# Block-sparse attention with an MLP behind it: the first batch's attention on float32 operands, and a planner with new numbers

## The chip, the core and the metric

The kernel runs on one core of a Trainium2 chip. The metric is device microseconds of one execution. The engines are TensorE (PE in the profile, with its weight loads as PEld), VectorE (DVE), ScalarE (ACT), GpSimd (POOL) and SyncE (SP), whose queue issues nearly all transfers.

## The reference

```python
scores = scale * np.matmul(q, k.transpose(0, 1, 3, 2))          # 4 batches, 8 heads, 768 positions, 64 wide
mask = |block_i - block_j| <= 1, first and last block row and column, 3 sampled blocks per block row
attn = softmax(np.where(mask, scores, -1e9))
attn_out = np.matmul(attn, v)
x = attn_out.transpose(0, 2, 1, 3).reshape(3072, 512)
h = x @ w_in                                                    # 512 x 2048
g = h * np.tanh(softplus(h))
return (g @ w_out).astype(np.float32)                           # 2048 x 512
```

A block has 32 positions, so a batch has 24 block rows. q, k and v are float32; the two weights arrive as 8-byte floats.

## The kernel before, in words

**Products in parts.** Every float32 operand of a large product is split into two float16 parts, a high one and a low one of what the high one leaves, after scaling by a power of two. A product is then three float16 products: high by high, low by high, high by low. The scale comes from a sum of squares: for the first batch from matmuls of a tile with itself (`gram`, L318) whose diagonal DVE picks (L333), for later batches from ACT squares (L309); a float32 matmul with a matrix of ones (`root_pe`, L344) sums over partitions, and DVE makes the scale (`root`, L349 and L352). `parts` writes the high part on ACT (L441) and the low part on DVE (L445).

**Attention.** A batch is 13 jobs: 11 of two sparse block rows each, and two dense ones (first and last block row). Per job: scores into PSUM (`scores`, L564; weights are 64x32 pieces of q, so eight such pieces lie side by side in the array), row maxima on DVE (L602 to L607), exponentials on ACT (L630), transposes on PE (L650), the transposed weights as high part on ACT (`ph`, L653) and low part on DVE (`pl`, L657), the product with v (`o_fn`, L679; 128x32 weights), then division (L698 to L701), a transpose (L708), and the parts of x (`xh` L726, `xl` L729). A sparse block row needs its keys gathered on POOL (`gather_k`, L504) and its values gathered by transfers (`gather_v`, L520 to L527) from `vd`, a copy of v in parts in device memory that `store_v` writes (L461). There are two value buffers (`vg`), so SP issues a gather when the block row two before it is done.

**Weights.** `w_in` comes in 8 transfers (`wr`), `w_out` in 16 (`wor`), all issued by SP (L745). DVE turns the 8-byte words into float32 with three integer operations per piece (L753, L756, L759). All of `w_out` has to be there before its one scale can be made (`scale_o`: `gram_wo`, `tp_wo`, `iv_o`); only then are its parts made (`parts_o`: `wt` L851 on DVE or L849 on ACT, high part L854 on ACT, low part L856 on POOL).

**MLP.** For 256 tokens `moe_h` (L895) makes h in groups of 12 matmuls and `moe_y` (L954) makes y in groups of 6. Between them lie `hs`, `us` and `g` (L904 to L939). The MLP has 192 groups of each; they are spread between the jobs. The first y group needs parts of `w_out`.

**What sets the order.** Every step is a `Task` with a planned duration, a priority `key` (smaller goes first) and a planned transfer time. `Plan.emit` (L85) plays the plan forward when the program is built and writes each engine's instructions in the order that it found; on the chip each engine then runs its list in that order. `pace` (L1099) holds a job's scores back: the first ones to the times in `START`, later ones so that the MLP keeps pace, with `RES` of it left for the end.

## Time and profile before

| | |
|---|---|
| three runs | 800.21, 801.33, 801.36 us |
| median | 801.33 us |
| profiled execution, span | 802.7 us (the page gives no time for it beside the span) |
| PE busy | 730.1 us, 91% of the span |
| DVE, ACT, POOL busy | 520.2, 536.2, 335.2 us |
| mean granted PE clock | 0.953 |
| moved | 94.22 MB |

Busy time is the time in which at least one instruction of a group is running, so groups that overlap in time add up to more than their engine's busy time. The mean of one matmul includes the time in which it overlaps its neighbours. "wr" and "wor" are raw pieces of the two weights, "raw_k" and so on raw tiles of the inputs.

### The profile page before, as it was taken

To read this page: it belongs to the slowest core of one execution; us is meant where nothing else is said; L and a number is where in the kernel's file an instruction comes from. 1 tells how busy PE (TensorE), PEld (TensorE's weight loads), DVE (VectorE), ACT (ScalarE), POOL (GpSimd) and SP (SyncE) were. 2 spreads that over 40 slices of the span, in tenths; PEclk is the share of its full clock that TensorE was granted. 3 is DMA by queue.
4 is the path that set the end of the run, shared out by engine and by line. 5 is a ranking of instruction groups with operands and counts; after the bars stand their busy time and mean duration, and the time that the engine had idled before them with its cause. 6 is when DMAs were issued, how large, how long until landed. Compare 5 with 4: busy or idle time off the path is not lost.

```text
span 802.7 us, 30250 instructions
## 1 busy us (share of the span) xinstructions
PE 730.1 (91%) x12626; PEld 515.6 (64%) x12626; DVE 520.2 (65%) x910; ACT 536.2 (67%) x836; POOL 335.2 (42%) x403
## 2 busy tenths in 40 slices
PE   4666678975999999999999999999999999999997
PEld 3544566763566757777677767677677767666653
DVE  6996777989786766767665666686767654323220
ACT  2556545777886748887777786886878766465650
POOL 2467540558674532434332543453545431302031
PEclk9956669997999999999999999999999999999999
DMA  8849557531304345526414264255243243100000
GB/s 286 311 136 242 148 151 228 185 108 41 120 36 148 87 112 156 144 88 188 135 57 121 79 173 138 69 148 151 61 128 93 80 136 89 39 14 14 15 14 26
DMA packets 56972, 94.22 MB, mean 117 GB/s; under 512 B 8067, under 2 KB 20356, under 8 KB 56836
## 3 DMA queue, kind: packets, MB, share of 16 engines
q1 hardware_dynamic: 56640, 92.03, 37.9%
q8 instruction: 99, 1.62, 0.9%
q14 instruction: 37, 0.30, 0.1%
q10 hardware_dynamic: 196, 0.27, 0.1%
HBM read 79.32 MB, written 12.95 MB: 115 GB/s over the span
## 4 chain that ended last, share of the span: by engine, by line
PE 72%; DVE 12%; DMA 7%; SPq 3%; issue 3%; ACT 2%; POOLq 0%; POOL 0%; DVEq 0%; ACTq 0%
PE y L954 28%; PE h L895 26%; PE t L650 6%; PE o L679 5%; PE s L564 5%; DMA wor<-in_moe_w_out_dram 2%; DMA wr<-in_moe_w_in_dram 1%; DVE wt L851 1%; SPq L527 1%; DMA vg<-vd 1%; PE tx L708 1%; DVE mx L607 1%; DVE wo L756 1%; DVE wi L756 1%; DMA vt<-vd 1%
## 5 line engine op out<-in xcount | busy, mean ns | idle before, releaser
L895 PE MATMUL h<-xh,wi 128*128 128x256 f16 x1536 | 286.6, 276 | 7.9 <-ACT hs L904 7.9
L954 PE MATMUL y<-wo,g 128*128 128x512 f16 x1152 | 278.4, 381 | 1.5 <-POOL g L939 0.9
L895 PEld LDWEIGHTS <-wi 128*128 128x128 f16 x2304 | 224.6, 99 | 61.2 <-issue 12.2
L895 PE MATMUL h<-xl,wi 128*128 128x256 f16 x768 | 211.5, 275 | 1.4 <-issue 1.4
L939 POOL TENSOR_TENSOR g<-hs,g 128x1024 f16<-128x1024 f32 x48 | 107.6, 2242 | 233.7 <-DVE g L936 146.0
L954 PEld LDWEIGHTS <-g 128*128 128x128 f16 x1152 | 110.3, 98 | 105.0 <-issue 5.1
L504 POOL COPY kg<-kt 128x256 f16 x264 | 121.5, 496 | 121.1 <-PE s L564 110.3
L904 ACT ACTIVATE hs<-h,gsc 128x512 f32<-128x512 f32 x96 | 65.6, 684 | 84.5 <-PE h L895 78.1
L630 ACT ACTIVATE pt<-s,nb,ns 128x256 f32<-128x256 f32 (+1 forms) x208 | 106.1, 579 | 8.0 <-PE t L650 4.0
L653 ACT ACTIVATE ph<-t 128x512 f16<-128x512 f32 x112 | 65.5, 593 | 62.9 <-PE t L650 50.3
L657 DVE SCALAR_TENSOR_TENSOR pl<-t,ph 128x512 f16<-128x512 f32 x112 | 76.0, 685 | 44.5 <-ACT ph L653 44.1
L928 DVE SCALAR_TENSOR_TENSOR hs<-us,hs 128x1024 f32<-128x1024 f32 x48 | 63.6, 1324 | 44.0 <-ACT us L927 42.2
L650 PE MATMUL t<-ident,pt 128*128 128x128 f32 x448 | 76.9, 299 | 12.9 <-ACT pt L630 5.8
L650 PEld LDWEIGHTS t<-ident,pt 128*128 128x128 f32 x448 | 56.1, 152 | 23.4 <-issue 4.8
L924 POOL TENSOR_TENSOR us<-us 128x1024 f32<-128x1024 f32 x23 | 46.9, 2041 | 54.7 <-DVE us L922 50.1
L679 PEld LDWEIGHTS <-ph 128*32 128x32 f16 x3584 | 50.7, 97 | 25.2 <-issue 19.9
L607 DVE TENSOR_REDUCE mx<-s 128x4 f32<-128x1024 f32 x44 | 53.4, 1213 | 7.4 <-PE s L564 7.3
L922 DVE TENSOR_SCALAR us<-us 128x1024 f32<-128x1024 f32 x48 | 38.8, 809 | 28.7 <-ACT us L918 28.6
L918 ACT ACTIVATE us<-hs,hsc 128x1024 f32<-128x1024 f32 x48 | 55.2, 1149 | 1.0
L926 ACT ACTIVATE us<-us 128x1024 f32<-128x1024 f32 x48 | 50.6, 1055 | 4.5 <-POOL us L924 3.8
L564 PEld LDWEIGHTS <-q 64*32 64x32 f16 x2976 | 35.6, 99 | 27.4 <-issue 22.3
L679 PE MATMUL o<-vg,ph 128*32 128x65 f16 (+1 forms) x3072 | 51.2, 201 | 2.1 <-DMA vg<-vd 2.0
(179 smaller groups left out, 895.3 us busy)
## 6 DMA issues: line engine op xcount, KB each, us to landing
...
wor<-in_moe_w_out_dram SPq DMA_DIRECT2D x16, 512.0 KB, 4.1
...
raw_k<-in_k_dram SPq DMA_DIRECT2D x12, 512.0 KB, 5.6
raw_q<-in_q_dram SPq DMA_DIRECT2D x12, 512.0 KB, 3.9
raw_v<-in_v_dram SPq DMA_DIRECT2D x12, 512.0 KB, 4.9
```

The lines of the kernel that those rows point to most:

```text
L504: nc.gpsimd.tensor_copy(out=kgs[n][:, :, c0:c0 + BS], in_=tl["kt", b][:, :, ds(j, BS)])
L564: nc.tensor.matmul(s[g][i * BS:(i + 1) * BS, c0 + cs.start:c0 + cs.stop], q[gs, c * NPR + i, qs], src[gs, a * NPR + i, ks], start=first an ...
L630: ex = lambda o, x, g, w: nc.scalar.activation(out=o, in_=x, func=AF.Exp, bias=nb[:, g, w:w + 1], scale=tl["ns", b, sus[w]["qb"] // TB][:, ...
L650: nc.tensor.transpose(t[:, k, g], src, ident)
L653: nc.scalar.activation(out=new(sb, "ph", ("ph", i, j), [P, 2, 2, P], F16), in_=tl["t", i, j], func=AF.Copy, scale=PSC)
L657: nc.vector.scalar_tensor_tensor(out=new(sb, "pl", ("pl", i, j), [P, 2, 2, P], F16), in0=tl["t", i, j], scalar=PSC, in1=tl["ph", i, j], op ...
L679: nc.tensor.matmul(o[cs, w, g, 0:v1 - v0], p[:, k, g, cs], vt[:, k, 2 * c + g, v0:v1], start=j == 0 and g == 0 and k == 0 and n == 0, stop ...
L895: nc.tensor.matmul(h[:, f2].rearrange("p (s q) -> p s q", q=BS), wi[:, fp, w, cc, fs], x[:, :, cc], start=f2 == 0 and k == 0, stop=f2 == 1 ...
L904: nc.scalar.activation(out=tl[kq][:, 2 * (fp % 2):2 * (fp % 2) + 2], in_=tl[kh], func=AF.Copy, scale=gsc[:, fp:fp + 1])
L928: add("DVE", 1.32, lambda: nc.vector.scalar_tensor_tensor(out=hs(), in0=us(), scalar=-0.5, in1=hs(), op0=ALU.add, op1=ALU.mult), r=[ku], w ...
L939: add("POOL", 2.3, lambda: nc.gpsimd.tensor_tensor(out=g()[:, 1], in0=hs(), in1=g()[:, 0], op=ALU.subtract), r=[kq, ("gh", b, t, k)], w=[kg])
L954: nc.tensor.matmul(tl[ky], tl["g", b, t, k][:, g, f, q], wo[:, fc, w], start=fc == 0 and n == 0, stop=fc == NFC - 1 and n == 2)
```

## The change

For batch 0 alone (`exact`), K and Q go straight into the tiles that the scores read, as float32 (`load32`); nothing is summed, scaled or split for them, and a constant stands in for their scale (`ns0`). The scores of a job are then 32 float32 matmuls for a sparse job, where 96 float16 ones were. V is copied as float32 beside a column of ones (`copy_v`) and stored as float32; a block row of v has the same bytes as before. The transposed weights are copied once as float32 (`pp`, on ACT or DVE) instead of `ph` and `pl`, and o is 16 float32 matmuls for 48. The scale of V is still needed for the MLP; its sum of squares is on ACT now. Batches 1 to 3 compute as before. The planned transfer times are lower (1.5 for 2.2 us, 3.0 for 4.4 us, 0.65 for 0.9 us), nearly every `key` has another number, `RES` exceeds the planned duration of the whole MLP, so `pace` holds back only the 18 jobs in `START`.

```diff
-RINGS = dict(s=1, t=2, o=1, h=2, y=1, raw=6, wr=3, pt=2, ph=4, pl=4, xh=3, xl=3, mx=3, nb=3, r=2,
+RINGS = dict(s=1, t=2, o=1, h=2, y=1, raw=6, wr=3, pt=2, pp=4, xh=3, xl=3, mx=3, nb=3, r=2,
...
-    vd = [dram.tile([S + BS, H, VW], F16, name=f"vd{b}") for b in range(B)]
+    exact = lambda b: b == 0
+    vd = [dram.tile([S + BS, H, D + 1 if exact(b) else VW], F32 if exact(b) else F16, name=f"vd{b}") for b in range(B)]
...
+    def load32(what, j):
...
+        def fn():
+            if what == "q" or j == 0:
+                t = new(sb, "kt" if what == "k" else "q", key, [P, NPR * (S if what == "k" else TT)])
+                tl[("x32", *key)] = full(t, k=S if what == "k" else TT)
+            dst = tl[("x32", *key)]
+            dst = dst[:, :, js] if what == "k" else dst
+            nc.sync.dma_start(out=dst, in_=(kT if what == "k" else qT)[b, :, :, js].rearrange("r d s -> d r s"))
+        first = what == "q" or j == 0
+        add("SP", 0.5, fn, w=[(what, b, j)], new=[("kt" if what == "k" else "q", key)] if first else (),
+            use=[key] if key not in ((what, b, j),) else (), key=-35, lat=2.0, kind=("dma", 1.5))
...
-            kind=("dma", 2.2 * n))
+            kind=("dma", 1.5 * n))
...
         first = what == "q" or j == 0
-        if b == 0:
-            if what == "q" or j == NTT - 1:
-                js = [j] if what == "q" else T3
-                add_gram((what, b, j), [lambda j=j: tl["flat", what, b, j] for j in js], [("raw", what, b, j) for j in js],
-                         "h", lambda: new(sb, f"ss{what}", key, [P, NTT])[:, 0:1], [key], [(f"ss{what}", key)], cls)
-            return
...
+    def copy_v(j):
+
+        key, kr = ("v", 0, j), ("raw", "v", 0, j)
...
+        def fn(eng):
+            dst, src = tl[key][:, :, :, 0:D], tl[kr].rearrange("p c (h d) -> p c h d", d=D)
+            if eng == "ACT":
+                nc.scalar.activation(out=dst, in_=src, func=AF.Copy)
+            else:
+                (nc.vector if eng == "DVE" else nc.gpsimd).tensor_copy(out=dst, in_=src)
+        add("POOL", 0.3, ends, w=[("ends",) + key], new=[("raw", key)], use=[key], key=-9)
+        add("DVE", 0.8, lambda: fn("DVE"), r=[kr, ("ends",) + key], w=[key], use=[key], key=ATV + 10,
+            also=[("ACT", 1.16, lambda: fn("ACT")), ("POOL", 2.0, lambda: fn("POOL"))])
...
-            r=[("v", b, j)], w=[("vd", b, j)], key=-4, lat=2.5, kind=("dma", 2.4))
+            r=[("v", b, j)], w=[("vd", b, j)], key=-6, lat=2.5, kind=("dma", 1.7))
...
+                kt, kg = (tl["x32", "kt", b], kg32) if exact(b) else (tl["kt", b], kgs)
+                nc.gpsimd.tensor_copy(out=kg[n][:, :, c0:c0 + BS], in_=kt[:, :, ds(j, BS)])
+        add("POOL", 0.53 * NR, fn, r=KT3(b) + ["off"], w=[("kg", n)], use=[("kt", b)], key=8)
...
-        add("SP", 2.9, fn, r=VD3(b) + ["off", "z"], w=[("vg", n)], key=-3, lat=2.4, kind=("dma", 0.9))
+        add("SP", 2.9, fn, r=VD3(b) + ["off", "z"], w=[("vg", n)], key=-2, lat=2.4, kind=("dma", 0.65))
...
-    WHOLE = 12
+    WHOLE = 13
...
+        if exact(b):
+            q = tl["x32", "q", b, qb // TB]
+            for m, (cs, src, ks) in enumerate(pieces):
+                for i in range(NPR):
+                    for g in range(2):
+                        gs = slice(g * D, (g + 1) * D)
+                        nc.tensor.matmul(
+                            s[g][i * BS:(i + 1) * BS, c0 + cs.start:c0 + cs.stop], q[gs, i, qs], src[gs, i, ks],
+                            start=first and m == 0, stop=last and m == len(pieces) - 1)
+            return
...
+        def pp_fn(j, eng):
+            pp_new(j)
+            if eng == "ACT":
+                nc.scalar.activation(out=tl["p32", i, j], in_=tl["t", i, j], func=AF.Copy)
+            else:
+                nc.vector.tensor_copy(out=tl["p32", i, j], in_=tl["t", i, j])
...
-            add("ACT", 0.62, lambda j=j: ph_fn(j), r=[kj], w=[("ph", i, j)], new=[("ph", ("ph", i, j))], key=-2.5)
-            add("DVE", 0.72, lambda j=j: pl_fn(j), r=[kj, ("ph", i, j)], w=[("pl", i, j)],
-                new=[("pl", ("pl", i, j))], key=-2.5)
+                key=72, lat=0.25, kind=("T", i))
+            kpp = ("pp", i, j)
+            if exact(b):
+                add("ACT", 0.62, lambda j=j: pp_fn(j, "ACT"), r=[kj], w=[("ph", i, j), ("pl", i, j)], use=[kpp],
+                    new=[("pp", kpp)], key=-53.5, also=[("DVE", 0.72, lambda j=j: pp_fn(j, "DVE"))])
+                continue
+            add("ACT", 0.62, lambda j=j: ph_fn(j), r=[kj], w=[("ph", i, j)], new=[("pp", kpp)], use=[kpp], key=46.5)
+            add("DVE", 0.72, lambda j=j: pl_fn(j), r=[kj, ("ph", i, j)], w=[("pl", i, j)], use=[kpp], key=-11.5)
...
+            if exact(b):
+                for g in range(2):
+                    for k in range(2):
+                        for c in range(NPR):
+                            cs = slice(c * BS, (c + 1) * BS)
+                            nc.tensor.matmul(
+                                o[cs, w, g, 0:D + 1], tl["p32", i, j][:, k, g, cs], vt[:, k, 2 * c + g],
+                                start=j == 0 and g == 0 and k == 0, stop=j == nt - 1 and g == 1 and k == 1)
+                return
...
-            add("PE", 0.46 * len(js), lambda js=js: [o_fn(j) for j in js],
+            add("PE", (0.6 if exact(b) else 0.46) * len(js), lambda js=js: [o_fn(j) for j in js],
...
+            if exact(b):
+                nc.vector.tensor_scalar(out=r, in0=o[:, 0:nsu, :, D], scalar1=1e-9, scalar2=iv_r, op0=ALU.add, op1=ALU.mult)
...
-        load(0, "k", [j])
-    load(0, "q", [0])
+        load32("k", j)
+    load32("q", 0)
...
     add("ACT", 1.0, lambda: which(new), w=["off", "z"],
-        new=[("raw", ("z",))], key=-9, lat=6.0)
-    for j in T3:
-        sums(0, "k", j, AT0)
-    scales(0, "k", 0, AT0)
-    sums(0, "q", 0, AT0)
-    scales(0, "q", 0, AT0)
-    for j in T3:
-        parts(0, "k", j, AT0)
-    parts(0, "q", 0, AT0)
+        new=[("raw", ("z",))], key=1, lat=6.0)
...
-        parts(0, "v", j, ATV)
+        copy_v(j)
         store_v(0, j)
...
+                if exact(b):
+                    load32("q", j)
+                    continue
...
-    RES, START = 145.0, [0, 33, 45, 57, 60, 66, 75, 66, 6, 3, 12, 30, 18, 12]
+    RES, START = 1694, [524, 191, 517, 34, 557, 53, 805, 8, 0, 613, 67, 118, 45, 152, 5, 146, 204, 169]
```

The new numbers move instructions. Three places matter. First DVE's list from behind the 20 rows on sampled blocks. Here `gram`, `iv`, `sc` and `ns` are the steps of a scale, `kt` and `q` the operand tiles, `mx` the row maxima. Before:

```order
L333 SCALAR_TENSOR_TENSOR gram_k_2_155,ss_k_0_186<-gram_k_2_155,ident 128x128
L349 TENSOR_SCALAR iv_k<-tp_k_0_188 128x1
L352 TENSOR_SCALAR iv_k<-iv_k 128x1
L229 TENSOR_SCALAR sc_k_0_199<-iv_k 128x1
L333 SCALAR_TENSOR_TENSOR gram_q_0_190,ss_q_0_205<-gram_q_0_190,ident 128x128
L445 SCALAR_TENSOR_TENSOR kt_203<-raw_k_0_116,sc_k_0_199,kt_203 128x4x256
L349 TENSOR_SCALAR iv_0_222<-tp_q_0_207 128x1
L352 TENSOR_SCALAR iv_0_222<-iv_0_222 128x1
L229 TENSOR_SCALAR sc_q_0_221<-iv_0_222 128x1
L413 TENSOR_SCALAR ns_0_226<-iv_0_222,iv_k 128x1 x2
L445 SCALAR_TENSOR_TENSOR kt_203<-raw_k_1_145,sc_k_0_199,kt_203 128x4x256
L445 SCALAR_TENSOR_TENSOR kt_203<-raw_k_2_147,sc_k_0_199,kt_203 128x4x256
```

and now:

```order
L511 COPY v_0_149<-raw_v_0_159 128x16x64
L511 COPY v_1_151<-raw_v_1_161 128x16x64
L511 COPY v_2_155<-raw_v_2_165 128x16x64
L670 TENSOR_REDUCE mx_239<-s_185 128x2
L672 TENSOR_REDUCE mx_239<-s_0_0_194 128x1
L672 TENSOR_REDUCE mx_239<-s_0_1_195 128x1
L673 TENSOR_TENSOR mx_239<-mx_239 128x2
L854 TENSOR_SCALAR wi<-wr_167 128x1024
L857 SCALAR_TENSOR_TENSOR wi<-wr_167,wi 128x1024
L860 SCALAR_TENSOR_TENSOR wi<-wr_167,wi 128x1024
L854 TENSOR_SCALAR wi<-wr_169 128x1024
L857 SCALAR_TENSOR_TENSOR wi<-wr_169,wi 128x1024
```

The scales and low parts of K and Q are gone; three copies of V stand first, then the maxima of the first job and the first weight.

Second, SP's list around the store of V (`vd`) and the first gathers (`vg`). Before:

```order
L745 DMA wr_164<-in_moe_w_in_dram 128x4x512
L745 DMA wr_166<-in_moe_w_in_dram 128x4x512
L745 DMA wr_168<-in_moe_w_in_dram 128x4x512
L374 DMA raw_v_2_229<-in_v_dram 128x2x512
L374 DMA raw_q_1_334<-in_q_dram 128x4x256
L745 DMA wr_388<-in_moe_w_in_dram 128x4x512
L745 DMA wr_411<-in_moe_w_in_dram 128x4x512
L745 DMA wr_596<-in_moe_w_in_dram 128x4x512
L461 DMA vd_60<-v_0_243 128x2x1040
L461 DMA vd_60<-v_1_247 128x2x1040
L461 DMA vd_60<-v_2_688 128x2x1040
L479 DMA vg_111<-vd_60 32x1040 x2
```

and now:

```order
L398 DMA kt_120<-in_k_dram 128x4x256 x2
L416 DMA raw_v_2_165<-in_v_dram 128x2x512
L846 DMA wr_167<-in_moe_w_in_dram 128x4x512
L846 DMA wr_169<-in_moe_w_in_dram 128x4x512
L846 DMA wr_171<-in_moe_w_in_dram 128x4x512
L517 DMA vd_60<-v_0_149 128x2x520
L517 DMA vd_60<-v_1_151 128x2x520
L517 DMA vd_60<-v_2_155 128x2x520
L846 DMA wr_291<-in_moe_w_in_dram 128x4x512
L846 DMA wr_341<-in_moe_w_in_dram 128x4x512
L536 DMA vg_111<-vd_60 32x520 x2
```

The stores of V stood behind six pieces of `w_in`; they stand behind three now. Of the gathers of sparse block rows, 18 stand ahead of the last `wor` in both lists, and six before, seven now, ahead of the first; the loads of batch 1's K stood ahead of the first `wor` and now stand behind the last.

Third, DVE's list ahead of the scale of `w_out` (`iv_o`). Before, where `iv_o` has 252 rows ahead of it:

```order
L759 SCALAR_TENSOR_TENSOR wo<-wor_4521,wo 128x512
L922 TENSOR_SCALAR us_0_3_4645<-us_0_3_4645 128x1024
L759 SCALAR_TENSOR_TENSOR wo<-wor_4574,wo 128x512
L759 SCALAR_TENSOR_TENSOR wo<-wor_4595,wo 128x512
L928 SCALAR_TENSOR_TENSOR hs_0_2_4330<-us_0_2_4381,hs_0_2_4330 128x1024
L657 SCALAR_TENSOR_TENSOR pl_2_4902<-t_2_4754,ph_2_4829 128x512
L657 SCALAR_TENSOR_TENSOR pl_0_4953<-t_0_4822,ph_0_4898 128x512
L607 TENSOR_REDUCE mx_4965<-s_4904 128x4
L333 SCALAR_TENSOR_TENSOR gram_wo,am_wo<-gram_wo,ident 128x128
L936 CAST g_0_2_5034<-hs_0_2_4330 128x1024
L922 TENSOR_SCALAR us_1_0_4900<-us_1_0_4900 128x1024
L349 TENSOR_SCALAR iv_o<-tp_wo 128x1
```

and now, where it has 194:

```order
L1023 TENSOR_SCALAR us_0_2_2900<-us_0_2_2900 128x1024
L860 SCALAR_TENSOR_TENSOR wo<-wor_2749,wo 128x512
L860 SCALAR_TENSOR_TENSOR wo<-wor_2771,wo 128x512
L830 TENSOR_TENSOR xl_2_2739<-tx_2966,xh_2_2738 128x256
L1023 TENSOR_SCALAR us_0_3_2994<-us_0_3_2994 128x1024
L734 COPY pp_0_3046<-t_0_3002 128x512
L359 SCALAR_TENSOR_TENSOR gram_wo,am_wo<-gram_wo,ident 128x128
L1029 SCALAR_TENSOR_TENSOR hs_0_2_2797<-us_0_2_2900,hs_0_2_2797 128x1024
L675 TENSOR_REDUCE mx_3118<-s_3013 128x4
L734 COPY pp_1_3153<-t_1_3052 128x512
L1029 SCALAR_TENSOR_TENSOR hs_0_3_2955<-us_0_3_2994,hs_0_3_2955 128x1024
L375 TENSOR_SCALAR iv_o<-tp_wo 128x1
```

All 25 rows of `pl` that stood ahead of it are gone, and two copies `pp` are there. PE's list has 324 matmuls of h ahead of its first y before and 288 now; the scores of all 13 jobs of batch 0 and no later one stand ahead of it in both.

More of the change, by code (lines that the diff above doesn't have):

```diff
@@ L299, in attn_mish_kernel, with half, full, heads16 @@
     NKG = NVG = 2
-    kgs = [const.tile([P, 2 * NPR, KT], F16, name=f"kg{n}") for n in range(NKG)]
-    vgs = [const.tile([P, 2, H, VW], F16, name=f"vg{n}") for n in range(NVG)]
     RAW = H * VW
+    def half(t, **kw):
+        k, n = next(iter(kw.items()))
+        return t.bitcast(F16).rearrange(f"p (r {k}) -> p r {k}", **kw)
+    def full(t, **kw):
+        k, n = next(iter(kw.items()))
+        return t.rearrange(f"p (r {k}) -> p r {k}", **kw)
+    def heads16(t):
+        return t.bitcast(F16).rearrange("p (c h d) -> p c h d", h=H, d=VW)
+    def heads32(t):
+        return t.rearrange("p (c h d) -> p c h d", h=H, d=D + 1)
+    kgf = [const.tile([P, NPR * KT], F32, name=f"kg{n}") for n in range(NKG)]
+    vgf = [const.tile([P, RAW], F32, name=f"vg{n}") for n in range(NVG)]
+    kgs = [half(t, k=KT) for t in kgf]
+    kg32 = [full(t, k=KT) for t in kgf]
+    vgs = [heads16(t) for t in vgf]
+    vg32 = [heads32(t) for t in vgf]
+    ns0 = const.tile([P, 2], F32, name="ns0")
+    iv_r = const.tile([P, 1], F32, name="iv_r")
+    for n, sign in enumerate((1.0, -1.0)):
+        nc.gpsimd.memset(ns0[:, n:n + 1], sign / float(D) ** 0.5)
     T3 = range(NTT)
@@ L334, in diag @@
                                            accum_out=out())
-        add("DVE", 0.4, diag, r=[kg], w=w, new=new_, key=cls - 2)
+        add("DVE", 0.4, diag, r=[kg], w=w, new=new_, key=cls + 5)
     def root_pe(key, ss, apart):
@@ L395, in fn @@
             squares(tl["raw", what, b, j], tl[key][:, k:k + 1])
-        add("ACT", 1.28, fn, r=[("raw", what, b, j)], w=[key], new=[(f"ss{what}", key)] if first else (), key=cls)
+        add("ACT", 1.28, fn, r=[("raw", what, b, j)], w=[key], new=[(f"ss{what}", key)] if first else (), key=cls + 7)
     def scales(b, what, j, cls):
@@ L407, in fn @@
                 iv = sb.tile([P, 1], F32, name=f"iv{b}_{j}", tag="iv", bufs=2)
-            root(kp, sc, iv, SQ if b else 0)
+            root(kp, sc, iv, SQ)
+            if what == "v" and exact(b):
+                nc.vector.tensor_scalar(out=iv_r, in0=iv, scalar1=float(2.0 ** -13), scalar2=None, op0=ALU.mult)
             if q:
@@ L456, in parts, with ends @@
             new={"k": [("kt", kt)] if first else [], "q": [("q", key)], "v": []}[what],
-            use=use + ([key] if what != "k" else []), key=cls)
-        add("DVE", 1.3, lo, port=True, r=[kr, ks, kh], w=[key, ("done",) + key], use=use, key=cls)
+            use=use + ([key] if what != "k" else []), key=cls + 54)
+        add("DVE", 1.3, lo, port=True, r=[kr, ks, kh], w=[key, ("done",) + key], use=use, key=cls - 113)
+    def copy_v(j):
+        key, kr = ("v", 0, j), ("raw", "v", 0, j)
+        def ends():
+            vt = new(sb, "raw", key, [P, RAW])
+            tl[key] = heads32(vt)
+            nc.gpsimd.memset(tl[key][:, :, :, D:D + 1], 1.0)
+        def fn(eng):
[7 more added lines that the diff above has]
+            also=[("ACT", 1.16, lambda: fn("ACT")), ("POOL", 2.0, lambda: fn("POOL"))])
     def store_v(b, j):
@@ L609, in mx_fn @@
                     axis=AX.X, op=ALU.max)
-        add("DVE", 2.6 if dense else 1.27, mx_fn, r=[ks] + (k2 if dense else []), w=[kmx], new=[("mx", kmx)], key=-1.5)
-        wq = [slice(0, nsu)] if len(qts) == 1 else [slice(w, w + 1) for w in range(nsu)]
+        add("DVE", 2.6 if dense else 1.27, mx_fn, r=[ks] + (k2 if dense else []), w=[kmx], new=[("mx", kmx)], key=-114.5)
+        wq = [slice(0, nsu)] if len(qts) == 1 or exact(b) else [slice(w, w + 1) for w in range(nsu)]
+        NS = [] if exact(b) else [("ns", b, t) for t in qts]
         def nb_fn(eng):
@@ L865, in fn @@
             nc.vector.tensor_scalar(out=gsc, in0=iv_i, scalar1=rg, scalar2=-2.0 * GSC, op0=ALU.mult, op1=ALU.mult)
-        add("DVE", 0.7, fn, r=[("iv", k) for k in range(0, NFP, 2)], w=["gsc"], key=-3)
+        add("DVE", 0.7, fn, r=[("iv", k) for k in range(0, NFP, 2)], w=["gsc"], key=-18)
     def scales_b(b):
```

130 lines of the change are left out of this document (69 added, 61 removed).

## The prediction

> **What bounds the kernel now.** I read the table of stretches first. Columns: stretch, its length, busy time of PE, PEld, DVE, ACT and POOL with instruction counts, granted clock, DMA share, GB/s.
>
> ```profile
> 0.00:40.00 40.00, 21.82 (x404) 16.90 (x404) 31.52 (x75) 16.08 (x23) 13.78 (x29) 0.98 0.85 299
> 40.00:120.00 80.00, 54.28 (x1575) 42.49 (x1574) 62.25 (x120) 44.07 (x82) 49.17 (x59) 0.63 0.61 169
> 120.00:175.00 55.00, 44.99 (x909) 36.54 (x908) 45.31 (x74) 35.98 (x53) 19.12 (x13) 0.97 0.60 192
> 175.00:200.00 25.00, 16.63 (x198) 11.15 (x197) 24.72 (x36) 18.40 (x30) 19.76 (x14) 0.84 0.13 33
> 200.00:802.00 602.00, 592.34 (x9549) 408.52 (x9547) 356.38 (x607) 421.70 (x650) 233.37 (x290) 1.00 0.32 95
> ```
>
> From 200 us on PE is busy for 592.3 of 602 us: there the program is as long as its matmuls, and none of them is taken away. The other 62.3 us of idle PE lie before 200 us, where DVE is the busiest engine (139.1 of the first 175 us, 79%). Next I asked what ends that stage: rows of DVE, then PE, in order of time, and the chain of waits.
>
> ```profile
> 175.01 0.16 DVE L349 TENSOR_SCALAR iv_o<-tp_wo 128x1 int32<-128x1 int32 x1 [3.74 <-PE tp_wo L344]
> 181.75 1.47 PE L954 MATMUL y<-wo,g 128*128 128x512 f16 x6
> ...
> 189.09 6.15 DVE wt L851 x4
> 195.27 0.63 ACT wo L854
> 196.52 2.72 PE h L895 x12
> 202.40 1.31 PE h L895 x12
> 203.71 1.30 PE y L954 x6
> ```
>
> The scale of the second weight is there at 175.0 us, the first y follows, then PE waits for the weight's parts until 196.5 us and is full from there on. So the question is when `iv_o` comes. SP's rows in order of time show the second queue that leads there:
>
> ```profile
> 33.79 4.42 SPq L461 DMA_DIRECT2D vd<-v  x3
> ...
> 44.19 0.63 SPq L520 DMA_DIRECT2D vg<-vd  x1
> ...
> 128.64 0.38 SPq L520 DMA_DIRECT2D vg<-vd  x1
> 129.79 2.59 SPq L527 DMA_DIRECT2D vg<-vd  x3
> 132.49 1.05 SPq L745 DMA_DIRECT2D wor<-in_moe_w_out_dram  x1
> 133.63 0.38 SPq L520 DMA_DIRECT2D vg<-vd  x1
> 134.79 2.59 SPq L527 DMA_DIRECT2D vg<-vd  x3
> ...
> 148.96 2.73 SPq L745 DMA_DIRECT2D wor<-in_moe_w_out_dram  x3
> ```
>
> The gathers run from 44.2 us (first) to 133.6 us (18th), and the pieces of the second weight stand between and behind them; the last is issued by 151.7 us. One gather takes SP at least 3.7 us (128.64 to 132.38 us).
>
> **The change, part by part.** First DVE ahead of `iv_o`. Groups in the first 175 us (the last row: of the whole run), columns: shapes and count, busy time, mean ns, idle before:
>
> ```profile
> L657 DVE SCALAR_TENSOR_TENSOR pl<-t,ph 128x512 f16<-128x512 f32 x25 | 16.9, 682 | 1.5 <-ACT ph L653 1.5
> L607 DVE TENSOR_REDUCE mx<-s 128x4 f32<-128x1024 f32 x11 | 13.4, 1219 | 4.6 <-PE s L564 4.6
> L753 DVE TENSOR_SCALAR wo<-wor 128x512 int32<-128x512 int32 x16 | 9.9, 620 | 9.8 <-DMA wor<-in_moe_w_out_dram 9.8
> L445 DVE SCALAR_TENSOR_TENSOR q<-raw_q,sc_q,q 128x1024 f16<-128x1024 f32 x3 | 4.1, 1357 | 0.0
> L445 DVE SCALAR_TENSOR_TENSOR v<-raw_v,sc_v,v 128x1024 f16<-128x1024 f32 x3 | 4.0, 1370 | 0.0
> L445 DVE SCALAR_TENSOR_TENSOR kt<-raw_k,sc_k,kt 128x1024 f16<-128x1024 f32 x3 | 3.8, 1280 | 0.5 <-ACT kt L441 0.5
> L922 DVE TENSOR_SCALAR us<-us 128x1024 f32<-128x1024 f32 x5 | 3.4, 682 | 0.0
> L333 DVE SCALAR_TENSOR_TENSOR gram_q<-gram_q,ident 128x128 f32<-128x128 f32 x3 | 0.9, 292 | 0.3 <-PE gram_q L318 0.3
> ```
>
> Gone: 25 low parts of weights, 16.9 us; nine low parts of K, Q and V, 11.9 us; one of eleven maxima, which the new list has behind `iv_o`, 1.2 us; the five diagonals and the scales of K and Q, which I put at 5 us together (an estimate: a diagonal takes 0.29 us, and a scale has three or four steps of less). Added: three copies of V and two of the transposed weights; DVE has no such copy before `iv_o`, so by the nearest row, `us` (a plain pass over 128x1024, 0.68 us), 2.0 us, and by `pl` at 0.68 us for the other two, 1.4 us. Net 31.6 us less, 107.5 us left ahead of `iv_o`. If DVE's share stays 79%, `iv_o` comes at 136 us; if the 35.9 us in which it idled all remain, at 143 us.
>
> Then SP. V's copies need no scale. The eight input pieces ahead of them are 4 MB, 13.4 us at the 299 GB/s of the first row; the stores then stand behind three `wr` of 1 MB, 10 us more. With the wait for a third decoded weight piece I put the first gather at 31 us, 13 us earlier than now (an estimate; it can be 40 us where `wr` is late). The 18 gathers at 3.7 us and 16 `wor` issues of some 0.4 us take SP 73 us; as slow as now they take 89.4 us plus 2. So the last `wor` is issued between 104 and 122 us (131 with the late start). From there to `iv_o` it was 23.3 us, with DVE behind; at least a landing, three decodes and the sum remain, 12 us by these rows:
>
> ```profile
> wor<-in_moe_w_out_dram SPq DMA_DIRECT2D x16, 512.0 KB, 4.1
> L756 DVE SCALAR_TENSOR_TENSOR wo<-wor,wo 128x512 int32<-128x512 int32 x16 | 14.4, 907 | 0.1
> L759 DVE SCALAR_TENSOR_TENSOR wo<-wor,wo 128x512 int32<-128x512 int32 x16 | 13.1, 827 | 0.1
> ```
>
> That gives 116 to 145 us (154 at worst). The bytes set a floor: by 175 us 36 MB were moved (206 GB/s, in the rows of the next fence), which take 120 us at 299 GB/s. DVE's and SP's ways agree on 136 us; I take it: 39 us earlier.
>
> Third, PE. The change trades three float16 products for one float32 product. What one float32 matmul costs is not shown by a like row, but its form is:
>
> ```profile
> L344 PE MATMUL tp_q<-ss_q,ones x24: 167/250/373, 11.4 to 604.0; 128*128 128x1 f32 x24
> 201.80 0.60 PE t L650 x4
> 0.00:175.00 175.00, 18.78 (x1104) 13.32 (x1104) 0.81 0.66 206
> 0.00:175.00 175.00, 17.30 (x1152) 13.75 (x1152) 0.81 0.66 206
> 0.00:175.00 175.00, 23.84 (x200) 18.18 (x200) 0.81 0.66 206
> ```
>
> The program has 12 such sums of Q (3 tiles in 4 batches) and the trace 24 records, so a float32 matmul runs as two. The last three rows are the scores (L564), o (L679) and the `gram` sums (L318) in the first 175 us. Two records for three: if a record streams as fast as a float16 one, scores and o shrink by a third, 12 us less; if each takes twice as long, they grow by a third, 12 us more. I take the dearer end, as the transposes, also float32, take 0.15 us for 128 columns at full clock (second row), while an h matmul takes 0.11 us for 256 (1.31 us for 12). Gone are 72 of 200 `gram` matmuls, 8.6 us. So PE's work ahead of `iv_o` stays near its 121.1 us within 4 us, and fits 136 us, as it includes 54.3 us at a clock of 0.63. If the cover is gone, it costs up to the 12 us. The Trainium skill, page "FP8 and Floating Point Precision", section "TensorE Precision Notes", says that true float32 takes four passes; by it the work is 4/3 of three products, the dear end, and the rows, with two records, leave it open whether each is two passes.
>
> ACT loses nine high parts and gains three squares of V; `pp` takes the place of `ph`. It was busy for 96 of 175 us and bounds nothing; the high parts hid behind DVE. Transfers carry the same bytes. Batch 1's K loads, now behind the last `wor`, are needed 13 jobs later and are hidden by h and y; without that cover they would cost one landing, some 6 us. The new priorities behind `iv_o` I cost at nothing: PE idles for 9.7 us there, so at most that is to be won, and the same again is my bound for a loss.
>
> Sum on the profiled span: `iv_o` 39 us earlier moves the full stretch as much. The new list has 36 h matmuls fewer ahead of the first y, 36 by 0.11 us is 4 us to be done later. 802.7 - 39 + 4 = 767.7 us. The span is 1.4 us above the median of the runs, so 766 us. From `iv_o` at 120 and at 154 us come 750 and 784 us, with 5 us either way for the rest 745 to 789.
>
> **Rivals.** *PE bounds the front.* Its list is in order, it had 53.9 us of idle before 175 us, and if half of that stays on top of 124 us, `iv_o` comes at 151 us: 781 us. For it: the clock of 0.63; against it: a fuller PE had 0.97 in the next row. *SP's queue runs at its floor,* `iv_o` at 116 us: 747 us. For it: 3.7 us per gather is all that SP itself takes; against it: the bytes leave no room for this. *Float32 pieces do not run side by side.* Now eight 64x32 pieces do. If float32 ones go one by one at the transposes' 0.15 us per 128 columns and record, 704 records of sparse scores take 106 us, the dense ones 29 us, 896 records of o at half the width 68 us: 203 us for 36.1. PE's front is then 121.1 - 8.6 - 36.1 + 203 = 279 us, `iv_o` 104 us later, the time 909 us. It makes the kernel slower once scores and o cost over 2.7 times as much (98 us). For it: no row shows a float32 matmul in a piece of the array; against it: both records of `tp_q` look like ordinary ones. The Trainium skill, page "TensorEngine Tiling (Array Packing)", section "Tile-to-Partition Mapping", bars float32 transposes from column pieces, not float32 products; no row here shows either. *The change moves nothing:* if the transfers alone set `iv_o`, it stays near 171 us and the 4 us of h eat the rest, 801 us. Against it: DVE waited only 9.8 us for `wor`.
>
> **Chances.** Forecast, `iv_o` at 120 to 150 us: 0.63. PE bounds the front: 0.18. The floor: 0.06. No difference, within 0.2% (1.6 us, about what a measurement of this kernel can tell): 0.03. Float32 pieces one by one, at any price past the turning point: 0.10. Faster thus 0.87. The range of the forecast, 745 to 789, takes in both neighbours and leaves out 0.13 to 0.2.
>
> **What would show it.** First gather near 31 us; `iv_o` near 136 us; no idle PE of over 3 us behind some 160 us; DVE busy for about 107 us ahead of `iv_o`; scores of batch 0 as 768 records and o as 896, at four thirds of the PE time at like clock. If the float32 groups cost more than twice that, or SP's first gather stays at 44 us, the prediction is wrong at that step. If `iv_o` comes early and the time does not follow, the new order behind it is at fault.

## The result

Before: median 800.77 us (799.37 to 801.36, four runs). After: median 777.38 us (775.31 to 778.63, four runs). The ratio is 0.969, with a 95% interval of 0.9651 to 0.9729: faster by 23 us. The forecast was 766 us, its range 745 to 789.

### The profile page after: what moved, and what is told of

It is laid out like the page before. It is cut to its first block, busy times and chain, and to the rows that moved or that the text cites. A ratio compares the mean times of both kernels' runs of the same rounds, so it can differ in the third digit from the quotient of the medians.

```text
span 774.5 us, 28498 instructions
## 1 busy us (share of the span) xinstructions
PE 713.9 (92%) x11766; PEld 503.1 (65%) x11766; DVE 483.6 (62%) x849; ACT 528.6 (68%) x827; POOL 332.3 (43%) x404
## 4 chain that ended last, share of the span: by engine, by line
PE 76%; DMA 10%; DVE 4%; SPq 3%; ACT 3%; issue 2%; POOLq 1%; POOL 0%; ACTq 0%; DVEq 0%
PE y L1055 30%; PE h L996 28%; PE t L721 6%; PE o L776 5%; PE s L632 4%; DMA vg<-vd 3%; DMA raw_q<-in_q_dram 2%; DMA vd<-v 2%; DMA wr<-in_moe_w_in_dram 1%; PE tx L809 1%; SPq L545 1%; DMA wor<-in_moe_w_out_dram 1%; SPq L585 1%; DVE us L1023 1%; PE o L766 1%
## 5 line engine op out<-in xcount | busy, mean ns | idle before, releaser
L996 PE MATMUL h<-xh,wi 128*128 128x256 f16 x1536 | 283.7, 274 | 1.3 <-ACT hs L1005 0.7
L562 POOL COPY kg<-kt 128x256 f16 (+1 forms) x264 | 119.8, 489 | 98.2 <-PE s L632 57.2
L701 ACT ACTIVATE pt<-s,nb,ns 128x256 f32<-128x256 f32 (+1 forms) x208 | 104.1, 579 | 13.1 <-PE t L721 10.3
L721 PE MATMUL t<-ident,pt 128*128 128x128 f32 x448 | 73.6, 288 | 6.3 <-ACT pt L701 2.4
L741 DVE SCALAR_TENSOR_TENSOR pp<-t,pp 128x512 f16<-128x512 f32 x84 | 56.1, 683 | 17.2 <-ACT pp L738 16.9
L721 PEld LDWEIGHTS t<-ident,pt 128*128 128x128 f32 x448 | 53.2, 146 | 18.7 <-issue 4.1
L738 ACT ACTIVATE pp<-t 128x512 f16<-128x512 f32 x84 | 48.5, 594 | 18.1 <-PE t L721 17.9
L1027 ACT ACTIVATE us<-us 128x1024 f32<-128x1024 f32 x48 | 50.8, 1058 | 4.9 <-POOL us L1025 4.1
L1028 ACT ACTIVATE us<-us 128x1024 f32<-128x1024 f32 x48 | 50.8, 1058 | 1.4
L776 PEld LDWEIGHTS <-pp 128*32 128x32 f16 x4032 | 37.2, 94 | 11.3 <-issue 10.5
L1037 DVE CAST g<-hs 128x1024 f16<-128x1024 f32 x32 | 28.9, 902 | 17.1 <-PE y L1055 16.4
```

What stands on the lines that cost most here:

```text
L562: nc.gpsimd.tensor_copy(out=kg[n][:, :, c0:c0 + BS], in_=kt[:, :, ds(j, BS)])
L701: ex = lambda o, x, g, w: nc.scalar.activation(out=o, in_=x, func=AF.Exp, bias=nb[:, g, w:w + 1], scale=ns(w)[:, 0:1])
L721: nc.tensor.transpose(t[:, k, g], src, ident)
L741: nc.vector.scalar_tensor_tensor(out=tl["pl", i, j], in0=tl["t", i, j], scalar=PSC, in1=tl["ph", i, j], op0=ALU.mult, op1=ALU.subtract)
L776: nc.tensor.matmul(o[cs, w, g, 0:v1 - v0], p[:, k, g, cs], vt[:, k, 2 * c + g, v0:v1], start=j == 0 and g == 0 and k == 0 and n == 0, stop ...
L996: nc.tensor.matmul(h[:, f2].rearrange("p (s q) -> p s q", q=BS), wi[:, fp, w, cc, fs], x[:, :, cc], start=f2 == 0 and k == 0, stop=f2 == 1 ...
```

## The profile after

The page's summary of the changed kernel: span, PE's busy time, and the granted clock in 40 equal slices.

```profile
span 774.5 us, 28498 instructions
PE 713.9 (92%) x11766; PEld 503.1 (65%) x11766; DVE 483.6 (62%) x849; ACT 528.6 (68%) x827; POOL 332.3 (43%) x404
PEclk9976999999999999999999999999999999999999
```

The span is 28.2 us shorter. PE's busy time is 16.2 us shorter and its idle time 12.0 us (72.6 to 60.6). The table of stretches says where; columns as in the prediction (busy time of PE, PEld, DVE, ACT, POOL; granted clock; DMA share; GB/s). First the changed kernel:

```profile
40.00:80.00 40.00, 26.31 (x595) 19.13 (x594) 26.11 (x51) 18.14 (x35) 29.48 (x35) 0.70 0.75 208
80.00:120.00 40.00, 30.00 (x621) 24.08 (x622) 28.72 (x60) 21.02 (x40) 18.58 (x26) 0.96 0.66 197
160.00:200.00 40.00, 37.84 (x419) 24.64 (x417) 34.01 (x48) 34.44 (x52) 30.18 (x29) 1.00 0.26 80
240.00:774.00 534.00, 526.61 (x8507) 366.64 (x8491) 300.83 (x526) 370.52 (x567) 200.57 (x241) 1.00 0.32 94
```

And the same stretches of the kernel before:

```profile
40.00:80.00 40.00, 24.64 (x751) 19.09 (x750) 32.04 (x57) 23.79 (x43) 28.08 (x33) 0.63 0.70 188
80.00:120.00 40.00, 29.64 (x826) 23.40 (x825) 30.21 (x64) 20.28 (x39) 21.09 (x27) 0.63 0.51 149
160.00:200.00 40.00, 27.09 (x408) 19.51 (x407) 35.98 (x50) 29.02 (x47) 28.02 (x17) 0.85 0.26 75
240.00:802.00 562.00, 552.34 (x9082) 383.24 (x9080) 324.45 (x559) 387.73 (x601) 204.83 (x255) 1.00 0.33 97
```

Two things changed. Between 160 and 200 us PE now idles for 2.2 us where it idled for 12.9: 10.7 of the 12.0 us of idle time. And from 80 to 120 us its clock is 0.96 where it was 0.63, though it is busy for nearly the same time. To put a number on the clock I multiplied busy time by granted clock in windows of 2 us over the whole span and added up: that is PE's work counted at the full clock, and what is left of the busy time is lost to the half clock.

| | before | after |
|---|---|---|
| PE's work at the full clock | 702.4 | 703.0 |
| lost to the half clock | 27.6 | 10.9 |
| PE idle | 72.6 | 60.6 |
| span | 802.7 | 774.5 |

PE's work is the same. Of the 28.2 us, 16.7 come from the clock and 12.0 from idle time. (For kernels with the same PE instructions, the runs below, the first row came out between 697 and 704 us, so each entry is good to some 4 us.)

The milestones of the prediction in the changed kernel: rows of SP (first gather, 18th gather, last piece of `w_out`), of DVE (`iv_o`) and of PE (first y), in order of time.

```profile
30.66 0.63 SPq L578 DMA_DIRECT2D vg<-vd  x1
...
118.70 0.38 SPq L578 DMA_DIRECT2D vg<-vd  x1
119.85 2.60 SPq L585 DMA_DIRECT2D vg<-vd  x3
122.56 0.84 SPq L846 DMA_DIRECT2D wor<-in_moe_w_out_dram  x2
```

```profile
146.64 0.15 DVE L375 TENSOR_SCALAR iv_o<-tp_wo 128x1 int32<-128x1 int32 x1
```

```profile
157.31 1.03 PE L1055 MATMUL y<-wo,g 128*128 128x512 f16 x4
```

The first gather came 13.5 us earlier, as predicted, but the 18 gathers still take 88.0 us from first to last (89.4 before). `iv_o` is 28.4 us earlier, not 39.

What a float32 product costs can be read at the full clock, from the start of a group to the start of what follows it. In the kernel before, one sparse job's scores (96 records) and one half of an o (48 records):

```profile
146.10 0.24 PE L564 MATMUL s<-kt,q 64*32 64x96 f16 x8
...
147.07 0.66 PE L650 MATMUL t<-ident,pt 128*128 128x128 f32 x4
```

```profile
130.06 0.25 PE L679 MATMUL o<-vg,ph 128*32 128x65 f16 x8
...
130.55 0.28 PE L895 MATMUL h<-xh,wi 128*128 128x256 f16 x1
```

The same in the changed kernel (64 and 32 records):

```profile
94.40 0.40 PE L622 MATMUL s<-kt,q 64*32 64x96 f32 x16
...
95.54 0.28 PE L996 MATMUL h<-xh,wi 128*128 128x256 f16 x1
```

```profile
97.88 0.66 PE L766 MATMUL o<-vg,pp 128*32 128x65 f32 x32
98.48 0.28 PE L996 MATMUL h<-xh,wi 128*128 128x256 f16 x1
```

Scores take 1.14 us for 0.97, o 0.60 us for 0.49: 1.18 and 1.22 times three float16 products, and side by side in the array as before.

## The experiments

All runs in one table. "Clock" is what PE lost to the half clock, "work" its busy time at the full clock, both reckoned as above, from the profiled execution; "clock", "work" and "idle" add up to the span. The ratio of each run is to the kernel before as measured beside it (800.8 to 802.1 us).

| run | median us | ratio to before (95%) | `iv_o` at | idle | clock | work |
|---|---|---|---|---|---|---|
| before | 800.77 | | 175.0 | 72.6 | 27.6 | 702.4 |
| after | 777.38 | 0.9651 to 0.9729 | 146.6 | 60.6 | 10.9 | 703.0 |
| e1 float32, old numbers | 792.94 | 0.9862 to 0.9917 | 122.9 | 67.7 | 23.9 | 701.2 |
| e2 float16, new numbers | 816.71 | 1.0153 to 1.0227 | 168.0 | 86.0 | 30.4 | 698.7 |
| e3 no sampled gathers | 774.40 | 0.9638 to 0.9691 | 131.7 | 57.6 | 14.8 | 701.0 |
| e4 two decodes of three | 775.91 | 0.9655 to 0.9712 | 116.8 | 60.1 | 12.7 | 702.3 |
| e5 `wor` on ACT's queue | 777.44 | 0.9681 to 0.9752 | 146.8 | 57.8 | 18.3 | 698.0 |
| e6 more matmuls | 791.04 | 0.9826 to 0.9899 | 165.0 | 59.7 | 15.7 | 719.5 |
| e7 more matmuls, old numbers | 813.33 | 1.0106 to 1.0177 | 143.6 | 70.3 | 18.0 | 724.3 |
| e8 old start table | 793.85 | 0.9856 to 0.9913 | 137.7 | 68.0 | 26.7 | 698.4 |
| e9 new start table alone | 825.46 | 1.0272 to 1.0307 | 142.8 | 89.1 | 30.0 | 704.4 |
| e10 no sampled transfers | 762.01 | 0.9469 to 0.9516 | 133.7 | 50.5 | 15.2 | 697.1 |
| e11 register loads first | 771.99 | 0.9630 to 0.9681 | 143.1 | 55.0 | 15.1 | 698.7 |
| e12 both e5 and e11 | 776.91 | 0.9669 to 0.9749 | 146.9 | 57.3 | 15.2 | 702.1 |

### The two halves of the change apart (e1, e2)

e1 is the changed kernel with the old priorities, transfer times, `RES` and `START`; `WHOLE` and one dependency of the dense scores stay as changed.

```diff
-    RES, START = 1694, [524, 191, 517, 34, 557, 53, 805, 8, 0, 613, 67, 118, 45, 152, 5, 146, 204, 169]
+    RES, START = 145.0, [0, 33, 45, 57, 60, 66, 75, 66, 6, 3, 12, 30, 18, 12]
...
-            use=[("kt", b)], key=76, lat=0.25, kind=("S", i))
+            use=[("kt", b)], key=-3, lat=0.25, kind=("S", i))
```

> The float32 attention of batch 0 alone: all keys, planned transfer times, RES and START as before. Theory A (the float32 path carries the gain: less work on VectorE, gathers begun at about 31 us): 778 to 790 us, iv_o by 155 us. Theory B (the new numbers carry it): within 5 us of 801 us, iv_o later than 165 us.

e2 is the kernel before with the new numbers on its float16 parts (the same lines the other way round).

> The new numbers alone on float16 parts: keys, planned transfer times, RES and START of the change, the sums and parts of batch 0 as before. Theory A (the float32 path carries the gain): 795 to 803 us, first gather still later than 40 us. Theory B (the new numbers carry it): 775 to 785 us.

Beside the kernel before at 802.11 us: 792.94 us with the float32 path alone, 9 us faster; 816.71 us with the new numbers alone, 15 us slower. Neither lies in a range that a theory gave it. Both together are 23 us faster. The two do not add up: the numbers help on the float32 path's steps and hurt on the float16 ones. e1 and the changed kernel have the same 11766 PE records; of the 18.2 us between their spans, 13.0 are clock and 7.1 idle time. And e1 has `iv_o` at 122.9 us, 24 us earlier than the changed kernel, yet is 16 us slower. An early `iv_o` alone buys little. SP's rows show what e1 pays for it: only 10 gathers stand ahead of its last `wor`, which is issued by 105.4 us, where the changed kernel has 18; its first gather comes at 46.3 us and its 18th at 140.1 us (30.7 and 118.7 in the changed kernel).

### Two queues to `iv_o`, each made shorter (e3, e4)

e3 leaves out the three sampled value transfers, with their register loads, for 20 of the 22 sparse block rows of batch 0 (stale values stand there instead).

```diff
-            for k, c0 in slots(su):
+            for k, c0 in slots(su) if b or su["ng"] < 2 else ():
                 j = block_at(nc.sync, "v", offv, k, S)
```

> The changed kernel without the three sampled value gathers (register loads and transfers) of 20 of the 22 sparse block rows of batch 0; stale rows stand in the value buffer, so the output differs. It takes 52 us of instructions off SyncE's queue ahead of the last wor, and no work off VectorE. Theory SP (the front of the changed kernel is as long as SyncE's list): iv_o falls from 146.6 us to 125 us or less, 750 to 758 us. Theory DVE (VectorE's list sets iv_o): iv_o moves by less than 5 us, 772 to 778 us.

e4 leaves out one of DVE's three integer operations on each piece of `w_out`; the planner made its lists anew without them.

```diff
-        for n in range(3) if wide else ():
+        for n in (range(3) if raw[0] == "wr" else (0, 2)) if wide else ():
```

> The changed kernel with two of the three integer operations on each piece of w_out (the middle one is left out, so w_out is wrong): 13 us less VectorE work ahead of iv_o, SyncE's list as it was. Theory SP: iv_o within 5 us of 146.6 us, 772 to 778 us. Theory DVE: iv_o 10 to 14 us earlier, 762 to 768 us.

774.40 and 775.91 us. No theory held: `iv_o` moved by 15 and by 30 us, and the time by 3 and 1.5 us at most. So an earlier `iv_o` did not bring the time with it. What moved `iv_o` in e4 is not shown: its expectation took SP's list to stay as it was, and it did not. The last two pieces of `w_out` and the 18th gather of e4:

```profile
96.57 0.84 SPq L846 DMA_DIRECT2D wor<-in_moe_w_out_dram  x2
...
132.99 0.32 SPq L578 DMA_DIRECT2D vg<-vd  x1
```

The last `wor` is issued 26 us earlier than in the changed kernel, with 12 gathers ahead of it and not 18, and the 18th gather 14 us later. As in e1, `iv_o` gained what the gathers lost. e3 has the lists of the changed kernel, but leaving out the loads moved them: a register that batch 0 loads is used again in batch 1, and with batch 0's loads gone batch 1 had to load. e3 idles for 13.8 us behind 240 us, the changed kernel for 7.4. e10 below separates the two.

### Another queue, and more work for PE (e5, e6, e7)

```diff
-        nc.sync.dma_start(out=raw.rearrange("p (c f) -> p c f", c=w.shape[1]) if len(w.shape) == 3 else raw, in_=w)
+        eng = nc.scalar if tag == "raw" else nc.sync
+        eng.dma_start(out=raw.rearrange("p (c f) -> p c f", c=w.shape[1]) if len(w.shape) == 3 else raw, in_=w)
```

> Edit: the changed kernel with the loads of `w_out`'s raw pieces issued on ACT's queue in place of SP's; lists otherwise as they are. The sampled value gathers and these loads no longer share a queue, so SP has some 20 us less to issue between 60 and 123 us. Theory 'the SP queue paces the front': gathers come sooner, the 18.7 us in which PE waits for `vg` ahead of 180 us fall by half, and the time falls by 5 to 9 us, to 768-772 us. Rival 'whatever the front gains is given back behind it' (as when the sampled gathers were left out, -1 us for 15 us, or the decode was cut, -1.5 us): `iv_o` earlier by up to 15 us and the time 774 to 778 us, with PE idle for longer behind 200 us.

777.44 us, no different, and `iv_o` where it was. ACT's list, too, is in order: it issued the pieces from 62.5 us on and the last by 120.2 us (123.4 in the changed kernel). SP had more time, the 18th gather came at 115.4 us (118.7), and SP's waits for PE rose. The waits of SP from 25 to 150 us that PE's `o` ended (us in total, times, longest), first the changed kernel, then e5:

```profile
SPq L578 <- PE o L766: 2.4, 2, 1.2
```

```profile
SPq L578 <- PE o L766: 10.9, 8, 4.1
```

So not the queue's length alone paces the gathers: a gather that SP could issue earlier waits for a value buffer, which `o` has to release, and `o` waits for the gather before.

e6 adds 64 float32 matmuls ahead of each sparse job's first `o` in batch 0, e7 adds the same to e1.

```diff
+            if exact(b) and not dense and j == 0:
+                for n in range(4):
+                    for g in range(2):
+                        for c in range(2 * NPR):
+                            cs = slice(c % NPR * BS, (c % NPR + 1) * BS)
+                            nc.tensor.matmul(o[cs, 0, g, 0:D + 1], tl["p32", i, j][:, n % 2, g, cs], ident[:, 0:D + 1],
+                                             start=True, stop=True)
             if exact(b):
```

> Edit: the changed kernel with 64 float32 matmuls more (onto the accumulator that the next real matmul clears) ahead of each sparse job's first `o` matmuls of batch 0; nothing waits for them, the output is the same. 11 jobs by 64 records at 0.65 us per 32 is 14 us of PE time at the full clock. Theory 'the granted clock of the front is set by how steadily PE is fed': PE's wait for `vg` is filled, the granted clock of 40 to 80 us rises from 0.70, and the 8 us that the low clock costs there pay for part of the 14 us: 772 to 779 us. Rival 'PE's work ahead of the first y is what counts and the clock is no lever': the clock of 40-80 us stays near 0.70 and the time rises by 8 to 14 us, to 785-791 us.

> Edit: the same added matmuls in the kernel that has the float32 path with all the old numbers (792.9 us; granted clock 0.71 from 40 to 120 us, PE busy 725.0 us against 713.9 us of the changed kernel for the same 11766 records). Theory of the clock: the granted clock from 40 to 120 us rises to 0.85 or more, and the added 14 us are paid back: 785 to 795 us. Rival 'the clock is no lever': the clock stays within 0.05 of 0.71, and the time rises to 800-807 us.

My size was off by two: a float32 matmul is two records, so 1408 records were added. Groups of e6 in the first 200 us (busy time, mean ns, idle before):

```profile
L766 PE MATMUL o<-ident,pp 128*32 128x65 f32 x1408 | 26.9, 238 | 7.7 <-issue 7.7
```

e6 took 791.04 us, 13.7 us more than the changed kernel, and e7 813.33 us, 20.4 us more than e1. In e6 the clock from 40 to 80 us rose to 0.88 but fell to 0.80 from 80 to 120 us, and the whole loss to the half clock grew (10.9 to 15.7 us); in e7 it shrank by 6 us, far less than the work that was added (its clock from 40 to 80 and 80 to 120 us was 0.71 and 0.83). e7 is outside both its ranges, and e6 at the upper end of its rival's. This way of filling PE does not pay. What e6 does show: PE idles for some 50 us before 240 us in both kernels (52.7 in the changed one, 50.2 in e6), so next to none of the added work went into that idle time. PE's waits for `vg` fell (18.7 to 8.5 us), but SP's waits for `o` from 25 to 150 us rose (2.4 to 18.5 us), and `iv_o` moved from 146.6 to 165.0 us. The added matmuls stand ahead of `o` in PE's list, so they fit the picture of a loop in which PE is itself a link.

### Which of the new numbers (e8, e9)

```diff
-    RES, START = 1694, [524, 191, 517, 34, 557, 53, 805, 8, 0, 613, 67, 118, 45, 152, 5, 146, 204, 169]
+    RES, START = 145.0, [0, 33, 45, 57, 60, 66, 75, 66, 6, 3, 12, 30, 18, 12]
```

e8 has this line in the changed kernel; e9 has the reverse of it in e1.

> Edit: the changed kernel with the old table of PE start times and the old reserve (`RES, START`), all its other new numbers kept. Theory 'the start table feeds PE': START decides at which point the planner puts each job's scores, and with them the `h` matmuls, into PE's list; without it PE waits and runs at the half clock as in the float32 kernel with all old numbers (busy time lost to the low clock 23.9 us there, 10.9 us in the changed kernel): 788 to 795 us. Rival 'the priorities and transfer times of the other engines feed PE': 775 to 781 us. If neither part works alone: over 785 us here and over 788 us in the next run.

> Edit: the float32 path with all the old numbers (792.9 us) and only the start table and the reserve of the changed kernel. Theory 'the start table feeds PE': 775 to 783 us, loss to the low clock near 11 us. Rival 'the other numbers feed PE': 789 to 796 us. If neither part works alone, it can also be slower than 796 us.

793.85 us without the new table, 825.46 us with the table alone, the slowest of all. e8 is where the theory of the start table put it, e9 is 42 us above its range. So the third case holds: neither part works alone. In e8 the loss to the half clock is back at 26.7 us and the idle time at 68.0.

### The gathers again, with the loads left in place (e10)

```diff
                 j = block_at(nc.sync, "v", offv, k, S)
                 p0 = c0 % P
-                nc.sync.dma_start(out=vg[p0:p0 + BS, c0 // P], in_=vd[b][ds(j, BS)])
+                if b or su["ng"] < 2:
+                    nc.sync.dma_start(out=vg[p0:p0 + BS, c0 // P], in_=vd[b][ds(j, BS)])
```

> Edit: the changed kernel without the same sampled value transfers of batch 0 as the run without sampled gathers (values of 20 block rows missing from the result), but with their register loads left where they are, so that batch 1's gathers keep the registers they had. Theory 'PE's gain ahead of 160 us is given back behind 200 us because the fixed lists then wait for other engines': 772 to 776 us again, PE idle behind 240 us 11 to 14 us (7.4 in the changed kernel, 13.8 in the run without sampled gathers). Rival 'the idle time behind 240 us came from the register loads that moved into batch 1': PE idle behind 240 us near 7.5 us, and the time 766 to 771 us.

762.01 us: 15 us faster than the changed kernel, 12 us faster than e3, with the same transfers left out, and below both ranges. My theory from e3, that the fixed lists give a gain in the front back later, fell. The last rows of the stretches, first e3, then e10, show PE idle for 13.8 and 7.7 us:

```profile
240.00:773.00 533.00, 519.22 (x8246) 360.64 (x8243) 293.45 (x509) 359.64 (x552) 196.23 (x229) 0.99 0.32 92
```

```profile
240.00:762.00 522.00, 514.26 (x8239) 357.78 (x8237) 292.17 (x509) 358.86 (x550) 195.08 (x229) 1.00 0.32 94
```

The edits differ in nothing but the register loads of batch 0, and SP's rows of batch 1 show where these went. In e3 a gap of 0.8 us stands between the window's transfer and the sampled ones, room for loads, in e10 one of 0.2 us:

```profile
236.13 0.32 SPq L578 DMA_DIRECT2D vg<-vd  x1
237.22 2.97 SPq L585 DMA_DIRECT2D vg<-vd  x3
240.29 1.18 SPq L578 DMA_DIRECT2D vg<-vd  x1
242.25 2.93 SPq L585 DMA_DIRECT2D vg<-vd  x3
```

```profile
224.14 0.32 SPq L578 DMA_DIRECT2D vg<-vd  x1
224.65 1.97 SPq L586 DMA_DIRECT2D vg<-vd  x3
226.72 0.36 SPq L578 DMA_DIRECT2D vg<-vd  x1
227.27 2.87 SPq L586 DMA_DIRECT2D vg<-vd  x3
```

From the first start to the last end these two gathers take 4.06 and 4.89 us in e3, and 2.48 and 3.42 in e10; between 205 and 300 us every gather has the gap of its kernel. How the slower gathers reach PE is not shown row by row: behind 240 us only 1.6 us of PE's waits in e3 are put down to `vg`. e10 also shows what the sampled transfers of batch 0 are worth in the front: PE's waits for `vg` fall, up to 160 us, from 18.7 to 3.5 us (changed kernel, then e10):

```profile
PE o L766 <- DMA vg<-vd: 18.7, 12, 5.4
```

```profile
PE o L767 <- DMA vg<-vd: 3.5, 4, 1.9
```

`iv_o` comes 13 us earlier there, at 133.7 us, and here the time does follow. The reading that fits is that the loop feeds PE with work and the early `iv_o` is only its sign. e10 does not take the loop apart, though: it leaves out the issue of 60 transfers on SP, their landing and their bytes at once. 60 of 65 KB are 3.9 MB, 13 us at the 299 GB/s of the first 40 us of the kernel before (an estimate), so fewer bytes are a rival that no run tests; against it, the DMA share of the changed kernel from 40 to 120 us was 0.75 and 0.66.

### A shorter way round the loop (e11, e12)

The waiting instruction of a gather is its window transfer; the register loads stand behind it. Ahead of it, they can run while SP waits.

```diff
             vg = (vg32 if exact(b) else vgs)[n]
+            at = {k: block_at(nc.sync, "v", offv, k, S) for k, _ in slots(su)} if exact(b) else {}
             nc.sync.dma_start(out=vg[a0:a1, 0], in_=vd[b][w0 * BS:w1 * BS])
```

e12 adds the edit of e5.

> Edit: the changed kernel with the three register loads of each value gather of batch 0 ahead of its window transfer, which waits until PE's `o` has released the buffer, and not between its transfers; nothing else moves. Without the sampled transfers, but with their register loads, the time was 762.0 us; so what stands between the release of a buffer and the landing of its last transfer is worth up to 15 us. Theory 'the loop from release through issue and landing back to `o` paces the front': the loads leave the loop where SP waits for the release, and 3 to 8 us are gained: 769 to 774 us. Rival 'SP's whole issue time paces it, waits or not': nothing leaves SP's queue, 776 to 779 us.

> Edit: the same, with the raw pieces of `w_out` also issued from ACT's queue (alone that gave 777.4 us, with 10.9 us in which SP waits for `o` to release a value buffer). Theory 'loop': SP has time to be at the loads before the release comes, so the whole of the three loads leaves the loop: gain of 6 to 12 us against the changed kernel, 765 to 771 us. Rival 'SP's whole issue time paces it': 772 to 778 us, since SP's queue is shorter but nothing in a gather is. Third way: the sampled transfers themselves (landing) and not their issue are what the loop waits for: 776 to 779 us in both runs.

771.99 us and 776.91 us. PE's waits for `vg` up to 160 us fell in both (to 13.9 and 12.1 us). e11 is in the range of the loop theory and 5 us below the changed kernel, but its interval (0.9630 to 0.9681) overlaps that of the changed kernel (0.9651 to 0.9729), so the gain is likely and not shown. e12, from which the same theory expected more, gave nothing: it lies in the ranges of the rival and of the third way, and counts against the theory. Both kernels with `wor` on ACT's queue have `iv_o` at 146.8 or 146.9 us, whatever their gathers do; in both, ACT issues the last pieces at the same time, by 120.2 us. Whether that holds `iv_o` there was not tried.

## Why the prediction was right, and where it was wrong

**Right, as read from rows.** These are of the changed kernel: the stretch ahead of `iv_o`, DVE's two groups of copies (count, busy time, mean ns), and PE's longest wait behind 160 us.

```profile
0.00:146.60 146.60, 97.72 (x1927) 74.55 (x1928) 105.89 (x202) 77.83 (x133) 74.44 (x100) 0.90 0.77 240
```

```profile
L511 DVE COPY v<-raw_v 128x1024 f32<-128x1024 f32 x3 | 2.1, 695 | 5.7 <-DMA raw_v<-in_v_dram 5.7
L734 DVE COPY pp<-t 128x512 f32<-128x512 f32 x3 | 2.0, 675 | 0.0
```

```profile
PE o L766 <- DVE pp L734: 1.3, 1, 1.3
```

First gather at 31 us: 30.66; it took both halves of the change, as it came at 46.3 us in e1 and 48.7 us in e2. DVE's time ahead of `iv_o`, 107.5 us: 105.89. V's copies and `pp` on DVE at 0.68 us each: 0.695 and 0.675. Float32 matmuls as two records, 768 for the scores and 896 for o. Their price at the dear end, 4/3: 1.18 to 1.22 at the full clock, so even a little below. The Trainium skill, page "FP8 and Floating Point Precision", section "TensorE Precision Notes", has four passes for true float32; by count alone that gives an estimate of 4/3, and the rows lie 8 to 12% below it. No wait of PE over 3 us behind 160 us: the longest is 1.3 us. The rival of float32 pieces one by one is refuted by the same rows.

**Mis-sized: "DVE's and SP's ways agree on 136 us; I take it."** `iv_o` came at 146.6 us. DVE's share did not stay at 79%: 105.89 of 146.60 us are 72%. SP's way came out at its slow end twice. The gathers kept their pace, 88.0 us for 18 (89.4 written down as the slow end), so that the last piece of `w_out` was issued by 123.4 us; and from there to `iv_o` it took 23.2 us, as before (23.3), not 12. The slow end of the prediction, 145 us, was thus nearly met; it chose between the ends by DVE's share, which says what DVE has to do and not what it waits for. e5 shows that the number of issues on SP's queue is not what holds the gathers. e10 points at the loop of gather, landing, `o` and release: without most of its transfers `iv_o` comes at 133.7 us and the time is 15 us shorter. That it is the loop, and not the bytes, is argued from the waits and not shown, and e12 speaks against it.

**Wrong as a cause: "`iv_o` 39 us earlier moves the full stretch as much."** In the changed kernel `iv_o` moved by 28.4 us and the span by 28.2. That looks like proof and is not. In e1 `iv_o` moved by 52 us and the span by 10; in e4 by 58 and the span by 27.6. The end follows more nearly how much of its work PE has behind it when it is full. At the full clock it had done 150.1 us of work by 240 us before and 176.3 after, 26 us more. e1 had done 156.1 us, e4 176.8. That is not all: e9 had done 153.5 us and e3 186.8, and both lost time behind 240 us, where PE idled for 23.3 and 13.8 us (7.4 in the changed kernel).

**Missing: the clock.** I counted 54.3 busy us at a clock of 0.63 as cover that would stay, and so had PE's work ahead of `iv_o` stay within 4 us of 121.1 us. By the row above it was 97.72 us, and PE was idle for 48.9 us there, hardly less than the 53.9 before. 16.7 of the 28.2 us are lost less to the clock. **Missing: the order.** I costed "the new priorities behind `iv_o`" at nothing within 9.7 us. The new numbers as a whole are worth 16 us on the float32 path (e1 to after) and cost 15 us without it (e2). The float32 path is worth 9 us with the old numbers and 39 us with the new ones (e2 to after), so neither half has a worth of its own.

**The rival "PE bounds the front"** (781 us, `iv_o` at 151) was closer to 777.4 us than the forecast. e6 bears out half of it: work added to PE in the front comes back in the time, though PE idles for 50 us there. That the sum came out 11 us from the result was in part luck, as two errors met: the float32 path with the old numbers gave 9 us and not the 35 that I had for the whole, and the new order, which I had at nothing, gave the rest.
